# Sending the rows of maxima from ScalarE's queue, holding raw weights two tiles further ahead, and fixing the step of bulk loads, memory reads and input splits

## The chip, the cores and the metric

The kernel runs on one core of one Trainium2 chip. A core has five engines that run side by side and are ordered only by semaphores: TensorE (PE in the profile), VectorE (DVE), ScalarE (ACT), GpSimd (POOL) and SyncE (SP), which here issues DMAs. ScalarE has a DMA queue too. The metric is the device time of one execution in microseconds; lower is better.

## The reference

A gated sum of two branches over the same input `x` (2048 tokens of width 640, all float32): an attention with a compressive memory over four segments of 512 tokens, 32 heads of width 20, and a gated MLP of inner width 1728.

```python
g = sigmoid((x * gate_w).sum(-1, keepdims=True))
# branch a, for each segment s = 0..3, per head
p = softmax(qs @ ks.T * scale + mask)          # causal inside the segment
a_dot = p @ vs
a_mem = (phi(qs) @ M) / (phi(qs) @ z + 1e-6)   # phi(t) = t+1 if t>0 else exp(t)
o = sigmoid(beta) * a_mem + (1 - sigmoid(beta)) * a_dot
M, z = M + phi(ks).T @ vs, z + phi(ks).sum(rows)
a = concat(o) @ wo
# branch b
b = (silu(x @ w1) * (x @ w3)) @ w2
out = g * a + (1 - g) * b
```

## The kernel before, in words

**Numbers in parts.** Projections and MLP products keep near-float32 accuracy by splitting each operand into a high and a low part (`split`, line 110: ScalarE copies the high part, line 111, and VectorE or GpSimd subtracts for the low part, line 112) and doing three passes over each block of 128 columns (`PASSES`). For the attention scores, q and k are split into three bfloat16 parts (`parts`, line 246), stored to DRAM in the order that the score product wants, and loaded again two heads at a time.

**Dense work and attention side by side.** `attention()` is a generator that walks through 128 heads (4 segments of 32) and yields ten times for each head step `t`. In one step TensorE does the scores of head `t` (`s_unit`, three PSUM banks in turn, two buffers) for their row maxima, the transposed scores of head `t-3` (`st_unit`, tag `t`, two PSUM buffers), whose exp ScalarE takes straight from PSUM (line 565) and whose corner GpSimd masks (line 571), and for every fourth head the product with v (`pv_quad`). The scores of a pair of heads need their maxima as three extra rows of q: VectorE takes maxima (line 526), splits them into three parts (`max_parts`, lines 536 to 539), transposes them (`max_rows`, line 545), and a small DMA (line 546) writes them into rows 120 to 122 of the pair's q tile `qst`. The first transposed score of the pair (line 557), issued two head steps later, reads them.

The dense work (projections, MLP, memory, output product) is a list of generators, cut into segments with end steps `segs`. The main loop takes one step of the attention, adds the segment's mean cost per step to a credit, and runs dense steps, each of which yields its cost in ns, while the credit lasts. `braid(a, b, every, skip)` puts one step of `b` behind every so many steps of `a` and runs what is left of `b` at the end. `after(n, f)` runs `f` after `n` ticks; `tick()` is called ten times in a head step.

**Order on the engines.** TensorE runs exactly in program order. On every other engine and queue a planner orders the instructions by readiness in its own model of time, except those wrapped in `here(...)`, which are pinned behind the instruction of the same engine that stands just ahead of them in the program, and those pinned by `behind`. Each engine and each queue then works strictly in its order, so one that waits holds everything behind it.

**Weights.** All weights are a list of tiles of 128 x 640 in order of use. `w_load` (line 137) sends one from DRAM into one of two raw buffers (`NRAW = 2`, issue at line 141); `w_split` makes the two-part tile W in one of six buffers (`NW = 6`), ScalarE for the high part, GpSimd (VectorE for the first seven) for the low part. `clock["oldest"]` is the oldest tile still in use. After every dense step `w_step` may split the older raw tile once it is four or five steps old, and load the next one if its W would fit: `clock["next"] < oldest + NW`.

**The other names the change touches.** `split_x` (line 210) splits the input of segments 2 and 3 into X, five blocks of 512, one to a step. `load_pair` (line 492) loads q, k, and every eighth head v, for a pair three steps ahead. `o_sums` (line 594) starts, after a segment's last head, the load of the softmax sums (line 595), then `o_scale` (line 614), which inverts and splits them on VectorE and sends them to `rR`, and five `o_load`s (line 600), each several DMAs on SP, which fetch the attention output. `normalize` (line 636) multiplies it by the inverted sums and adds the memory's part (`gt`, from `load_memory`, line 628). `memory_read` (line 277) does the products `nd` of phi(q) with M in eight steps. `oproj` returns `first()`, five normalize steps and then the splits into `oT`, and `rest()`, the output product.

Of the kernel before, what the change touches and what calls it, by code (L numbers as in the profile page):

```python
# [17 lines left out]
P = 128  # L18
S, D, H, DH, NSEG, L = 2048, 640, 32, 20, 4, 512
# [3 lines left out]
VE = DH + 1  # L23
VG = 8 * VE
SCALE = DH ** -0.5
BIG = -1.0e38
NST, NW, NRAW, NHT, NVG, ND = 4, 6, 2, 6, 2, 3
KR = 6 * DH
LAG_T, LAG_P, NP, AGE, NO = 3, 4, 4, 4, 5
# [5 lines left out]
def gated_mix(ctx: ExitStack, tc: tile.TileContext, xT, wqk, wv, w13, w2, w2h, wo, beta, out):  # L35
    nc = tc.nc
# [8 lines left out]
    vd = [dp.tile([P, 4, H * VE], F32, name=f"vd{c}") for c in range(NSEG)]  # L45
# [51 lines left out]
    here = tc.keep_in_program_order  # L97
    last = {}
# [11 lines left out]
    def split(dst, src, lo=None, pin=lambda ins: ins):  # L110
        pin(nc.scalar.copy(dst[:, 0], src))  # L111
        (lo or nc.gpsimd.tensor_sub)(dst[:, 1], src, dst[:, 0].bitcast(F32))  # L112
# [4 lines left out]
    def ht_tile(shape, dt, name):  # L117
        return sp.tile(shape, dt, tag="hT", name=name, bufs=NHT)
# [10 lines left out]
    items, tiles = [], {}  # L129
# [21 lines left out]
    def w_step():  # L151


        clock["step"] += 1
        for r in raws:
            if clock["step"] - r[3] == (AGE // 2 if "exp" in last else AGE) and r[0] >= 7:
                r[4] = last.get("exp", last["act"])
        if raws and clock["step"] - raws[0][3] >= (AGE if "exp" in last or raws[0][0] < 7 else AGE + 1):
            w_split()
        if len(raws) < NRAW and clock["next"] < min(len(items), clock["oldest"] + NW):  # L160
            w_load()

    def w_get(i, oldest=None):
# [46 lines left out]
    def split_x(c):  # L210
        x_tile(c)
        for kb in range(KB):
            split(Xs[c][:, :, kb, :], xraw[c][kb], lo=nc.vector.tensor_sub)
            yield 1

    xraw = {}
# [29 lines left out]
    def parts(name, ps, phi=None):  # L246


        s = ht_tile([P, 3, L], BF, name)
        if phi is not None:  # L250
            e = f_tile("phi_t")
            nc.vector.tensor_scalar(e, ps, 0.0, None, op0=ALU.min)
        nc.scalar.copy(s[:, 0], ps)
        if phi is not None:
            nc.scalar.activation(e, e, AF.Exp)
        t = f_tile(f"{name}_t")
        nc.vector.tensor_sub(t, ps, s[:, 0])
        if phi is not None:
            nc.vector.scalar_tensor_tensor(phi, ps, 0.0, e, op0=ALU.max, op1=ALU.add)
        last["act"] = nc.scalar.copy(s[:, 1], t)  # L260
        nc.gpsimd.tensor_sub(s[:, 2], t, s[:, 1])
        return s
# [135 lines left out]
    def job_read(c):  # L398
        return 5.6, memory_read(c)
# [92 lines left out]
    def load_pair(j):  # L492

        c, h = divmod(j, H)
        q, k = qst[j // 2 % NST], kst[j // 2 % NST]
        for mb in {DH * h // P, (DH * h + 2 * DH - 1) // P}:
            assert ("q", c, mb) in stored and ("k", c, mb) in stored
        assert ("v", c, 3) in stored
        for t, src in ((q, qd[c]), (k, kd[c])):
            nc.sync.dma_start(t[:KR], src[DH * h:DH * h + 2 * DH].rearrange("(h d) a n -> (d a) h n", h=2))  # L500
        if h % 8 == 0:
            v = sp.tile([P, 4, VG + 12], F32, tag="vg", name=f"vg{j}", bufs=NVG)
            nc.gpsimd.memset(v[:, :, VG:], 0.0)
            nc.sync.dma_start(v[:, :, :VG], vd[c][:, :, VE * h:VE * h + VG])
            bank["v"] = v
        m = sp.tile([P, 8], F32, tag="m", name=f"m{j}", bufs=4)
        for i in range(2):
            o = VE * (h % 8 + i)
            heads[j + i] = dict(c=c, h=h + i, q=q[:, i], k=k[:, i], pair=q, v=bank["v"][:, :, o:o + 32], m=m)
# [32 lines left out]
    def max_rows(j):  # L542
        mr = sp.tile([32, P], BF, tag="mr", name="mr")
        for g in range(4):
            nc.vector.transpose(mr[:, 32 * g:32 * g + 32], heads[j]["ns"][32 * g:32 * g + 32])
        nc.sync.dma_start(heads[j]["pair"][KR:KR + 3].rearrange("a h (b n) -> a (h b) n", n=P), mr[:24])

    def st_unit(j, t):
        u = heads[j]
# [43 lines left out]

    def o_sums(c):
        here(nc.sync.dma_start(rs, od[c][:, DH].rearrange("h (a n) -> h a n", n=P)))
        after(4 if c < NSEG - 1 else 3, o_scale, c)
        for b in range(KB):
            after(1 + 3 * b if c < NSEG - 1 else 1 + b, o_load, c, b)

    def o_load(c, b):  # L600

# [26 lines left out]
    def load_memory(c):  # L628

        assert ("g", c, 3) in stored  # L630
        gms[c] = big_tile(f"gm{c}")[:, :4 * D].rearrange("p (b d) -> p b d", b=4)
        for qb in range(4):
            here(nc.sync.dma_start(gms[c][:, qb], gd[c][:, qb]))
            yield 1
# [20 lines left out]
    def after(n, f, *a):  # L655
        soon.append([n, f, a])
# [77 lines left out]
    def store(c, qb=None):  # L734
        o = out[0, c * L:(c + 1) * L, :].rearrange("(b p) d -> p b d", p=P)
        for qb in range(4):
            here(nc.sync.dma_start(o[:, qb], accs[c][:, qb]))
            yield 1
# [4 lines left out]
    def job_up(cs, j):  # L743
        return (4 if j < NF else 2) * 3.5, ffn_up(cs, j, plan_up([j])[0])
# [6 lines left out]
    def job_down(cs, g, last=False):  # L751
        return 2.384 * sum(3 if j < NF else 2 for j in GROUPS[g]), ffn_down(cs, GROUPS[g], plan_down(GROUPS[g]), last)

    def jobs_up(cs, g):
        return [job_up(cs, j) for j in GROUPS[g]]

    def jobs_group(cs, g):
        return [job_up(cs, j) for j in GROUPS[g]] + [job_down(cs, g)]
# [14 lines left out]
    def chain(jobs):  # L773
        return sum(c for c, _ in jobs), (y for _, g in jobs for y in g)

    def braid(a, b, every, skip=0):

        def gen():
            n = 0
            for y in a[1]:  # L780
                yield y
                n += 1
                if n > skip and (n - skip) % every == 0:
                    z = next(b[1], None)
                    if z is not None:
                        yield z
            yield from b[1]
        return a[0] + b[0], gen()

    A, B = (0, 1), (2, 3)  # L790
# [16 lines left out]

    seg = job_q2(A, 3)
    g = jobs_group(A, 0)
    seg += [braid(g[0], job_read(1), 2)] + g[1:] + jobs_group(A, 1) + jobs_up(A, 2)  # L810
    segs.append((H + LAG_P + 1, seg))
    d = job_down(A, 2)
    u = job_up(A, GROUPS[3][0])
# [8 lines left out]
    segs.append((2 * H - 3, seg))  # L822
    seg = job_q(B, 1) + job_q(B, 2)
    q = job_q2(B, 3)
    seg += q[:2] + [q[2], braid(q[3], job_read(2), 1)]
    segs.append((2 * H + LAG_P, seg))
    up = [job_up(B, 0), job_up(B, 1)]
    o1, o2 = jobs_oproj(1)
    seg = [braid(braid(up[0], job_read(3), 2), (0, load_memory(1)), 6), braid(up[1], o1, 2), o2, (0, store(1)), job_up(B, 2), job_down(B, 0)] + jobs_up(B, 1)
    segs.append((3 * H + LAG_P + 1, seg))  # L830
    d = job_down(B, 1)
    u = job_up(B, GROUPS[2][0])
    o1, o2 = jobs_oproj(2)
    seg = [braid(d, (0, load_memory(2)), 3), braid(u, o1, 2), o2] + [job_up(B, j) for j in GROUPS[2][1:]]
    seg += [job_down(B, 2), (0, load_memory(3))] + jobs_up(B, 3)
    segs.append((NJ + LAG_P, seg))
    d, u = job_down(B, 3), jobs_up(B, 4)
# [90 lines left out]
```

## Time and profile before

| | |
|---|---|
| median of 3 runs | 1187.81 us (1186.01 to 1189.77) |
| the profiled execution's own time | 1190.22 us |
| its span, first to last instruction | 1188.5 us |
| TensorE busy | 1151.5 us, 97% |
| VectorE / ScalarE / GpSimd busy | 681.0 / 495.0 / 458.1 us |
| mean granted TensorE clock | 0.991 |
| DMA | 151.87 MB, 128 GB/s on average |

How to read the lines that follow. Times are in us unless marked ns. A line of the waits names an engine and line of code, what it waited for, the us in total, how often, and the longest. A line of the order of time has start, length, engine, line, operation, output <- input and shape, and in brackets the idle time of that engine just before, and what ended it. A line of the stretches has the stretch, its length, then busy time and count of PE, PE's weight loads, VectorE, ScalarE and GpSimd, then the granted TensorE clock, the busy share of the DMA engines and GB/s. SPq is the queue of SP. TensorE's matmuls are pipelined, so a busy PE is not PE at its peak, but an idle one is idle. A wait for several semaphores is put down to the one that came last.

### The profile page before, as it was taken

The numbers are of one execution on the slowest core, as the hardware profiler recorded it, in microseconds if no ns is written. First come the engines' busy times: TensorE is split into PE (matmuls) and PEld (weight loads), VectorE is DVE, ScalarE is ACT, GpSimd is POOL, SyncE is SP. The second block draws the span as 40 slices with busy tenths as digits, with TensorE's granted clock in tenths as the row PEclk, the third lists the DMA queues.
The fourth block names the chain that finished last, engine by engine and source line by source line (L and its number), as shares of the span: only waits on it lengthen the run. The fifth ranks groups of instructions, "written<-read, shape, count | busy, mean of one in ns | idle before, by whom it ended". The sixth has DMA issues, their size and how long they took to land.

```text
span 1188.5 us, 20034 instructions
## 1 busy us (share of the span) xinstructions
PE 1151.5 (97%) x6953; PEld 875.6 (74%) x6953; DVE 681.0 (57%) x2183; ACT 495.0 (42%) x988; POOL 458.1 (39%) x574
## 2 busy tenths in 40 slices
PE   8999999999999999999999998999997999999998
PEld 6978766767767787877876665768666676776888
DVE  4033574466656655583365886765656776664454
ACT  6255334544342334343455633545542344334140
POOL 7065533244343335242265422342432325334250
PEclk9999999999999999999999999999998999999999
DMA  9375523233324244316377665342435324231212
GB/s 303 140 228 210 198 73 94 87 99 83 98 77 115 84 122 124 95 51 192 116 240 236 225 197 159 116 141 82 114 94 143 87 86 121 77 121 55 81 56 89
DMA packets 108213, 151.87 MB, mean 128 GB/s; under 512 B 12240, under 2 KB 69584, under 8 KB 108112
## 3 DMA queue, kind: packets, MB, share of 16 engines
q1 hardware_dynamic: 87760, 123.59, 34.7%
q10 hardware_dynamic: 20352, 27.01, 6.3%
q8 instruction: 54, 0.88, 0.3%
q14 instruction: 47, 0.39, 0.1%
HBM read 95.25 MB, written 54.53 MB: 126 GB/s over the span
## 4 chain that ended last, share of the span: by engine, by line
PE 82%; DVE 7%; DMA 4%; issue 3%; POOL 2%; ACT 1%; SPq 0%; POOLq 0%; DVEq 0%; ACTq 0%
PE g L224 15%; PE f L478 15%; PE u L224 14%; PE o L582 6%; PE v L325 6%; PE s L519 5%; PE op L718 5%; PE t L557 4%; PE k L224 4%; PE q L224 4%; DVE junk L526 2%; PE t L562 1%; DMA qst<-mr 1%; PE nd L291 1%; POOL W L112 1%
## 5 line engine op out<-in xcount | busy, mean ns | idle before, releaser
L526 DVE CUSTOM_DVE_ANT_0 junk<-s,mask 128x128 bf16<-128x128 f32 (+3 forms) x512 | 249.5, 487 | 220.7 <-PE s L519 213.0
L565 ACT ACTIVATE P<-t 128x384 f32<-128x384 f32 (+1 forms) x384 | 202.2, 527 | 351.7 <-PE t L557 137.7
L112 POOL TENSOR_TENSOR W<-wr,W 128x640 fp32r<-128x640 f32 (+1 forms) x126 | 197.2, 1571 | 171.2 <-ACT W L111 163.2
L571 POOL TENSOR_SCALAR_AFFINE_SELECT P<-P 128x256 f32<-128x256 f32 x256 | 105.1, 411 | 388.6 <-ACT P L565 377.4
L224 PE MATMUL g<-X,W 128*128 128x512 f32 x840 | 242.7, 424 | 0.0
L224 PE MATMUL u<-X,W 128*128 128x512 f32 x780 | 228.8, 429 | 1.0 <-DVE oall L643 1.0
L478 PE MATMUL f<-W,ht 128*128 128x320 f32 x1312 | 225.7, 323 | 2.9 <-DVE acc L483 2.6
L478 PEld LDWEIGHTS f<-W,ht 128*128 128x128 f32 x1312 | 201.7, 191 | 10.7 <-DVE acc L483 4.0
L224 PEld LDWEIGHTS g<-X,W 128*128 128x128 f32 x840 | 152.2, 190 | 26.8 <-issue 2.2
L224 PEld LDWEIGHTS u<-X,W 128*128 128x128 f32 x780 | 143.9, 192 | 25.6 <-DVE oall L643 1.4
L519 PE MATMUL s<-kst,qst 120*128 120x128 bf16 (+3 forms) x512 | 135.6, 306 | 1.2 <-DVE m L526 1.0
L111 ACT CAST W<-wr 128x640 fp32r<-128x640 f32 (+1 forms) x133 | 95.2, 724 | 67.9 <-PE f L478 21.7
L557 PE MATMUL t<-qst,kst 123*128 123x512 bf16 (+1 forms) x256 | 93.8, 366 | 10.4 <-DMA qst<-mr 9.6
L483 DVE SCALAR_TENSOR_TENSOR acc<-f,cgate,acc 128x320 f32<-128x320 f32 x128 | 70.0, 549 | 54.3 <-PE f L478 53.4
L112 POOL TENSOR_TENSOR ht<-ft,ht 128x512 fp32r<-128x512 f32 x52 | 67.8, 1304 | 74.5 <-ACT ht L111 73.7
L224 PE MATMUL q<-X,W 128*128 128x512 f32 x300 | 81.0, 414 | 3.7 <-POOL X L112 1.9
L519 PEld LDWEIGHTS <-qst 120*128 120x128 bf16 x512 | 44.3, 99 | 52.2 <-issue 44.2
L718 PE MATMUL op<-W,oT 128*128 128x320 f32 x480 | 82.7, 325 | 0.0
L224 PE MATMUL k<-X,W 128*128 128x512 f32 x300 | 80.7, 412 | 2.0 <-ACT mt L385 2.0
L325 PE MATMUL v<-W,X 128*128 128x320 f32 (+1 forms) x480 | 76.5, 317 | 1.8 <-POOL W L112 1.8
L582 PE MATMUL o<-P,vg 128*32 128x512 f32 (+3 forms) x1024 | 77.9, 443 | 0.3 <-POOL P L571 0.3
L718 PEld LDWEIGHTS op<-W,oT 128*128 128x128 f32 x480 | 73.8, 190 | 1.5 <-issue 0.4
(110 smaller groups left out, 1226.5 us busy)
## 6 DMA issues: line engine op xcount, KB each, us to landing
wr<-in_w_dram SPq DMA_DIRECT2D x80, 320.0 KB
qst<-qd SPq DMA_DIRECT2D x64, 240.0 KB
kst<-kd SPq DMA_DIRECT2D x64, 240.0 KB
od<-oq ACTq DMA_DIRECT2D x32, 256.0 KB
qd<-qs ACTq DMA_DIRECT2D x20, 384.0 KB
kd<-ks SPq DMA_DIRECT2D x20, 384.0 KB
wr<-in_wqk_dram SPq DMA_DIRECT2D x21, 320.0 KB
wr<-in_wo_dram SPq DMA_DIRECT2D x20, 320.0 KB
```

Of the source, the lines that this page charges most:

```text
L111: pin(nc.scalar.copy(dst[:, 0], src))
L112: (lo or nc.gpsimd.tensor_sub)(dst[:, 1], src, dst[:, 0].bitcast(F32))
L224: nc.tensor.matmul(ps, w[:, a, kb * P:(kb + 1) * P], x[:, b, kb, :], start=n == 0, stop=n == 14)
L325: nc.tensor.matmul(ps[:, :n1 - n0], x[:, a, kb, lb * P:(lb + 1) * P], wvt[kb][:, b, n0:n1], start=n == 0, stop=n == 14)
L478: nc.tensor.matmul(ps[:, :320], a, b, start=n == 0, stop=n == len(ms) - 1)
L519: nc.tensor.matmul(ps[:, o:o + n], q[:KR, qb * P:(qb + 1) * P], k[:KR, :n], start=qb != 1, stop=qb != 0, skip_group_check=True)
L526: nc.vector.tensor_tensor_reduce(out=junk[:, :n], in0=ps[:, o:o + n], in1=mask[:, L - n:], scale=1.0, scalar=-3.0e38, op0=ALU.add, op1=ALU ...
L557: nc.tensor.matmul(ps[:, :n], k[:KR + 3, t * P:(t + 1) * P], q[:KR + 3, t * P:], start=True, stop=True)
L565: last["exp"] = nc.scalar.activation(P32[:, o:o + n], src, AF.Exp, scale=SCALE)
L571: nc.gpsimd.affine_select(d, d, pattern=[[0, 2], [1, P]], base=0, channel_multiplier=-1, compare_op=ALU.is_ge, fill=0.0)
L582: nc.tensor.matmul(ps[32 * i:32 * i + 32, kb * P:], u["v"][:, kb], u["P32"][:, o:o + n], start=kb == 0, stop=kb == 3, skip_group_check=True)
L718: nc.tensor.matmul(ps[:, :320], oT[0][:, qb % 2, a, kb * P:(kb + 1) * P], ws[kb][:, b, 320 * hf:320 * hf + 320], start=n == 0, stop=n == 14)
```

## The change

- `max_rows`: the DMA of the rows is issued by ScalarE, pinned, six ticks after the transposes.
- `w_step`: raw tiles are loaded up to `NRAW` tiles beyond those whose W fits; the split now asks itself whether W fits.
- `split_x`: the ScalarE copies are pinned at their steps. `load_pair`: the loads of the first four pairs (`j < 8`) are pinned on SP.
- `parts`: ScalarE's copy stands ahead of VectorE's min in the program, for queries and keys with phi.
- `o_sums`: `o_scale` after 7 ticks, `o_load`s six ticks apart (first three segments).
- Segments: `job_read(1)` starts four steps later; `job_read(2)` leaves what does not fit to the next segment, whose first job takes it up ahead of `job_read(3)`, with another cost; `load_memory(1)` comes every five steps after eight; `load_memory(2)` moves ahead into the previous segment; `normalize(1)` starts two steps later and `normalize(2)` takes every third step in place of every second.

```diff
@@ w_step
-        if raws and clock["step"] - raws[0][3] >= (AGE if "exp" in last or raws[0][0] < 7 else AGE + 1):
+        if raws and raws[0][0] < clock["oldest"] + NW and \
+                clock["step"] - raws[0][3] >= (AGE if "exp" in last or raws[0][0] < 7 else AGE + 1):
             w_split()
-        if len(raws) < NRAW and clock["next"] < min(len(items), clock["oldest"] + NW):
+        if len(raws) < NRAW and clock["next"] < min(len(items), clock["oldest"] + NW + NRAW):
             w_load()
@@ split_x
-            split(Xs[c][:, :, kb, :], xraw[c][kb], lo=nc.vector.tensor_sub)
+            split(Xs[c][:, :, kb, :], xraw[c][kb], lo=nc.vector.tensor_sub, pin=here)
@@ parts
         s = ht_tile([P, 3, L], BF, name)
+        nc.scalar.copy(s[:, 0], ps)
         if phi is not None:
             e = f_tile("phi_t")
             nc.vector.tensor_scalar(e, ps, 0.0, None, op0=ALU.min)
-        nc.scalar.copy(s[:, 0], ps)
-        if phi is not None:
             nc.scalar.activation(e, e, AF.Exp)
@@ load_pair (q and k; the same for v)
-            nc.sync.dma_start(t[:KR], src[DH * h:DH * h + 2 * DH].rearrange("(h d) a n -> (d a) h n", h=2))
+            i = nc.sync.dma_start(t[:KR], src[DH * h:DH * h + 2 * DH].rearrange("(h d) a n -> (d a) h n", h=2))
+            if j < 8:
+                here(i)
@@ max_rows
-        nc.sync.dma_start(heads[j]["pair"][KR:KR + 3].rearrange("a h (b n) -> a (h b) n", n=P), mr[:24])
+        dst = heads[j]["pair"][KR:KR + 3].rearrange("a h (b n) -> a (h b) n", n=P)
+        after(6, lambda: here(nc.scalar.dma_start(dst, mr[:24])))
@@ o_sums
-        after(4 if c < NSEG - 1 else 3, o_scale, c)
+        after(7 if c < NSEG - 1 else 3, o_scale, c)
         for b in range(KB):
-            after(1 + 3 * b if c < NSEG - 1 else 1 + b, o_load, c, b)
+            after(1 + 6 * b if c < NSEG - 1 else 1 + b, o_load, c, b)
@@ braid
-    def braid(a, b, every, skip=0):
+    def braid(a, b, every, skip=0, rest=True):
...
-            yield from b[1]
+            if rest:
+                yield from b[1]
@@ segments
-    seg += [braid(g[0], job_read(1), 2)] + g[1:] + jobs_group(A, 1) + jobs_up(A, 2)
+    seg += [braid(g[0], job_read(1), 2, 4)] + g[1:] + jobs_group(A, 1) + jobs_up(A, 2)
...
-    seg += q[:2] + [q[2], braid(q[3], job_read(2), 1)]
+    r = job_read(2)
+    seg += q[:2] + [q[2], braid(q[3], r, 1, 0, False)]
...
-    seg = [braid(braid(up[0], job_read(3), 2), (0, load_memory(1)), 6), braid(up[1], o1, 2), o2, (0, store(1)), job_up(B, 2), job_down(B, 0)] + jobs_up(B, 1)
+    r = 0.37 * job_read(3)[0], chain([r, job_read(3)])[1]
+    seg = [braid(braid(up[0], r, 2), (0, load_memory(1)), 5, 8), braid(up[1], o1, 2, 2), o2, (0, store(1)), job_up(B, 2), job_down(B, 0), (0, load_memory(2))] + jobs_up(B, 1)
...
-    seg = [braid(d, (0, load_memory(2)), 3), braid(u, o1, 2), o2] + [job_up(B, j) for j in GROUPS[2][1:]]
+    seg = [d, braid(u, o1, 3), o2] + [job_up(B, j) for j in GROUPS[2][1:]]
```

More of the change, by code (lines that the diff above doesn't have):

```diff
@@ L503, in load_pair @@
             nc.gpsimd.memset(v[:, :, VG:], 0.0)
-            nc.sync.dma_start(v[:, :, :VG], vd[c][:, :, VE * h:VE * h + VG])
+            i = nc.sync.dma_start(v[:, :, :VG], vd[c][:, :, VE * h:VE * h + VG])
+            if j < 8:
+                here(i)
             bank["v"] = v
```

## The prediction

> **What bounds the kernel now.** I read the page first, then the waits of TensorE, then the granted clock around them, then the single instructions at each stall.
>
> ```profile
> span 1188.5 us, 20034 instructions
> PE 1151.5 (97%) x6953; PEld 875.6 (74%) x6953; DVE 681.0 (57%) x2183; ACT 495.0 (42%) x988; POOL 458.1 (39%) x574
> ```
>
> PE is busy for 97% of the span and the other engines for 57% at most. The matmuls are the same before and after, so the change can only win the time in which PE stands, or runs at half clock. TensorE's waits, longest first:
>
> ```profile
> PE t L557 <- DMA qst<-mr: 9.6, 2, 6.0
> PE f L478 <- DVE acc L483: 2.6, 2, 2.1
> PE nd L291 <- DVE fu L447: 2.6, 1, 2.6
> PE nd L291 <- DVE gm L299: 2.3, 2, 1.6
> ...
> PE v L325 <- POOL W L112: 1.8, 2, 1.2
> PE gt L647 <- DVE fu L447: 1.8, 2, 1.6
> ...
> PE s L519 <- DVE m L526: 1.0, 3, 0.7
> PE u L224 <- DVE oall L643: 1.0, 1, 1.0
> PE t L557 <- ACT P L565: 0.8, 1, 0.8
> ```
>
> These nine are 23.5 us. The largest is PE waiting for a row of maxima (mr) twice. Next, the busy time of the engines in five stretches; the figure before the last two is the granted clock:
>
> ```profile
> 526.30:529.70 3.40, 3.13 (x12) 3.13 (x13) 2.55 (x9) 0.73 (x1) 2.72 (x2) 0.50 0.32 94
> 703.80:707.20 3.40, 3.40 (x12) 2.41 (x12) 2.16 (x9) 0.93 (x2) 0.00 (x0) 0.50 0.68 200
> 720.90:724.30 3.40, 3.40 (x28) 1.17 (x24) 1.21 (x5) 0.00 (x0) 0.00 (x0) 0.50 0.81 281
> 912.00:918.80 6.80, 2.68 (x10) 2.41 (x11) 0.57 (x2) 0.00 (x0) 0.00 (x0) 0.50 0.98 262
> 942.70:946.10 3.40, 3.40 (x11) 2.29 (x10) 1.37 (x4) 0.38 (x1) 0.41 (x1) 0.51 0.27 88
> ```
>
> Each lies right behind (or over the end of) one of the stalls above. PE worked 3.13 + 3.40 + 3.40 + 2.68 + 3.40 = 16.0 us there at half clock, so 8.0 us were lost on top of the stalls. Stalls and half clock together, 31.5 us, are what this change could reach.
>
> **The change part by part.** The profiled execution took 1190.2 us, 2.4 above the median of the runs (1187.8); the sum is made against 1190.2 and 2.4 is taken off at the end.
>
> *Rows of maxima moved from SP's queue to ScalarE's.* The two late rows:
>
> ```profile
> 710.14 0.84 DVE L545 STREAM_TRANSPOSE mr<-ns 32x32 bf16<-32x32 bf16 x4
> 712.45 0.73 SPq L609 DMA_DIRECT2D oall<-od  x1
> 714.10 5.29 DMA qst<-mr
> 719.43 0.39 PE L557 MATMUL t<-qst,kst 123*128 123x512 bf16 x1 [3.59 <-DMA qst<-mr]
> 904.58 0.84 DVE L545 STREAM_TRANSPOSE mr<-ns 32x32 bf16<-32x32 bf16 x4
> 909.47 6.61 DMA qst<-mr
> 916.12 0.61 PE L557 MATMUL t<-qst,kst 123*128 123x512 bf16 x1 [6.03 <-DMA qst<-mr]
> ```
>
> The rows were ready at 710.98 and 905.42, but SP issued them at 714.10 and 909.47, behind a run of bulk loads. On ScalarE's queue they stand behind no bulk load. Their landing is bounded by two kinds of rows. The shortest from issue to first use:
>
> ```profile
> 741.96 0.72 SPq L546 DMA_DIRECT2D qst<-mr  x1
> 744.61 0.38 PE L557 MATMUL t<-qst,kst 123*128 123x512 bf16 x1
> ```
>
> is 2.65 us; with it both rows land at 713.6 and 908.1, before PE stood (715.84 and 910.09), and all 9.6 us go. With the 5.29 and 6.61 us of their own stretches they land at 716.27 and 912.03, 0.4 and 1.9 us remain, and 7.2 go. The bulk loads stay in those stretches, only thinner, so I take the middle, **8.4**. [...]
>
> The price is on ScalarE, which now issues 64 of them:
>
> ```profile
> L546 SPq DMA_DIRECT2D qst<-mr x64: 720/727/903, 151.1 to 1086.8; - x64
> 239.41 0.60 ACT L565 ACTIVATE P<-t 128x512 f32<-128x512 f32 x1 [1.03 <-POOL ht L112]
> 239.41 0.84 DVE L545 STREAM_TRANSPOSE mr<-ns 32x32 bf16<-32x32 bf16 x4
> 937.94 0.59 ACT L565 ACTIVATE P<-t 128x512 f32<-128x512 f32 x1
> 939.65 0.83 DVE L545 STREAM_TRANSPOSE mr<-ns 32x32 bf16<-32x32 bf16 x4
> ```
>
> 64 x 0.727 = 46.5 us of ScalarE's stream. Six ticks behind `max_rows` is the place right before the next `t` unit 0, so ScalarE issues the row before that unit's exp. I compared, for 63 pairs, that exp's start with the end of the transposes: in 26 of them (the first is the pair at 239) the rows are ready later, by 22.4 us in all and at most 2.5 us (940.48 against 937.94). In these ScalarE would stand, with that exp and everything behind it queued: the next exps, the tanh and the evacuations that VectorE waits for. Who needs that exp soonest is the matmul that takes its PSUM bank again, two units later:
>
> ```profile
> 653.36 0.60 ACT L565 ACTIVATE P<-t 128x512 f32<-128x512 f32 x1 [1.10 <-PE t L557]
> 657.20 0.23 PE L560 MATMUL t<-qst,kst 123*128 123x128 bf16 x1
> ```
>
> It has 657.20 - 653.96 = 3.2 us to spare, as much as the worst pair takes (2.5 + 0.73). So most is hidden. Ends: 0, and 26 x 0.73 + 22.4 = 41.4 if nothing hid it. PE waited for an exp once, for 0.8 us, so I stay near the lower end: **+3.0**. SP loses a wait: 64 rows no longer hold its queue, which delays nothing that PE waits for otherwise: 0.
>
> *X splits kept at set steps.* Five ScalarE copies of X3 now run in one burst when X's slot comes free, and the VectorE halves behind them hold back the evacuation:
>
> ```profile
> 521.59 2.78 DVE L112 TENSOR_TENSOR X<-xr,X 128x512 fp32r<-128x512 f32 x2
> 524.89 1.00 PE L478 MATMUL f<-W,ht 128*128 128x320 f32 x5 [2.14 <-DVE acc L483]
> ```
>
> With each copy pinned three steps after the last, two halves no longer meet. Between 0 and -2.6 I take the longer stall alone, **-2.1**.
>
> *Raw weights two tiles beyond.* 133 loads of 320 KB go up to two tiles earlier, and a split then follows as soon as its W slot is free, instead of load, five steps, split. The weights nearly never bind PE: 1.8 us for v, where five tiles are needed at once. **-1.8** (ends 0 and -1.8, and the row is that case).
>
> *`o_scale` at 7 ticks, `o_load`s six apart.* VectorE, in order, stood for the sums:
>
> ```profile
> DVE rs L616 <- DMA rs<-od: 4.5, 4, 1.7
> ```
>
> and the tanh product (fu), hence PE's 2.6 us for nd, came behind it. Three more ticks cover the 1.7: **-1.7** (ends 0, -2.6).
>
> *Memory reads later, memory loads earlier, normalize at every third step.* Starting `job_read(1)` four steps later removes the longer of the two gm waits: **-1.6** (ends 0, -2.3). Spacing `normalize(2)` wider removes gt and u, 2.8, in part: **-1.8**. But its `oT` splits then come at the very end of that up job, where before six steps lay between. The next product needs them:
>
> ```profile
> L111 ACT CAST oT<-oall x80: 287/297/325, 397.8 to 1163.5; 128x128 fp32r<-128x128 f32 x80
> ```
>
> The cost is between 0 and five copies and a VectorE half, about 1.8; the first matmul needs one copy behind one other ScalarE job, 0.3 + 0.6 + 0.3, so **+1.2**. `job_read(2)` leaves three of eight steps to the next segment but is paid in full in its own, so dense work ends some 2 us early there; an end without dense work cost PE the 0.8 (t) and 0.7 (s) above: **+0.8** (ends 0, 2.1). The next segment's pace is set 5.6 us too low and that work runs at its end; PE works either way: 0.
>
> *`parts`: ScalarE's copy before VectorE's min.* ScalarE no longer waits for phi_t in front of its exps; the t and s waits of 0.8 and 0.7 followed such a wait: **-1.5** (ends +0.8, -1.8). *Loads of the first four pairs pinned on SP*: nine transfers, with a lead of 30 ticks, 0.
>
> *Half clock.* 8.0 us, of which the stretches behind removed stalls go. **-5.0** (ends 0, -8.0), because not every stall goes. Here the half clock followed even the 2.1 us stall at 524.89. [...]
>
> *New order.* All engines but PE are planned anew, which can open waits like the 0.8 to 2.6 us ones above: **+3.0** (ends 0, 8).
>
> Sum: -8.4 - 2.1 - 1.8 - 1.7 - 1.6 - 1.8 - 1.5 - 5.0 = -23.9; +3.0 + 1.2 + 0.8 + 3.0 = +8.0; net -15.9. 1190.2 - 15.9 - 2.4 = **1172**.
>
> **The rivals.** *A, the small gains are given back.* VectorE's own delays stay:
>
> ```profile
> L537 DVE TENSOR_TENSOR nm<-m,ns x64: 103/168/1492, 147.5 to 1085.3; 128x8 f32<-128x8 f32 x64
> ```
>
> A 0.17 us operation took up to 1.49. The 126 weight splits on POOL remain, so the stalls of VectorE may only change place, and pins and steps do little. Then the rows alone gain: 8.4 + 3.0 of clock - 8.0 = 3.4, **1184**. Against it: four small stalls have an ordering cause that the change names. [...]
>
> *B, slower: ScalarE stands for the rows.* If the exp's 3.2 us of room is less elsewhere, all 41.4 us come to PE instead of 3.0: 1172 + 38 = **1210**. It decides from about 19 us exposed, under half of it. For it: 26 pairs come late. Against it: ScalarE is busy for 42%, and only one pair reaches the room.
>
> *C, slower: raw loads block SP.* A raw load waits for POOL to free the raw tile, with the next pairs' q and k behind it:
>
> ```profile
> SPq L141 <- POOL W L112: 186.7, 60, 16.1
> ```
>
> A pair is loaded three steps ahead, 22 us by the first and last start of the mr issues (935.7 / 63 = 14.9 us for two steps). If earlier loads double the longest wait, to 32, a pair is 10 late, with a half-clock stretch 11.7; three of them give **1207**. It decides from two such waits. Against it: today's longest is 6 us short of one.
>
> **How the numbers follow.** Forecast 0.54, with its own range 1163 to 1181; A 0.24; B 0.12; C 0.10. About 0.3% (1184.2 to 1191.4) is what a measurement of this kernel can tell from no change. A lies at that edge: 0.16 faster, 0.08 same. So faster 0.70, same 0.08, slower 0.22. Outside 1160 to 1198 lie B (0.12), half of C (0.05) and 0.03 below.
>
> **What would show it.** Right: PE's wait for mr under 2.4 us, no half clock at 720 and 912, PE's waits for acc and v gone, ScalarE's issues of mr near 0.73 us each. Wrong: exps standing behind mr (B), SP waiting over 22 us for POOL and PE for qst or kst (C), PE waits of the old total under other names (A).

## The result, and the profile after

| | before | after |
|---|---|---|
| median in the comparison | 1190.63 us (1186.01 to 1194.15) | 1179.38 us (1175.83 to 1180.61) |
| the profiled execution's own time | 1190.22 us | 1179.5 us |
| its span | 1188.5 us | 1177.5 us |
| mean granted TensorE clock in it | 0.991 | 0.996 |

The ratio after to before is 0.9903, with a 95% interval from 0.9875 to 0.9931: 11 us faster. The forecast was 1172, so the sign and the range held. The time is 7.4 us above the forecast, and 2.8 of these are no part of the change: the sum took 2.4 us off because the median of three runs was 1187.81, and over six runs the kernel before has 1190.63. Counted as a change, 15.9 us were forecast and 11.2 measured. From the page of the changed kernel, its span and the engines' busy time:

```profile
span 1177.5 us, 20041 instructions
...
PE 1148.4 (98%) x6953; PEld 874.2 (74%) x6953; DVE 684.9 (58%) x2183; ACT 495.5 (42%) x988; POOL 456.4 (39%) x574
```

The waits of TensorE in the changed kernel (what it waited for, us in total, how often, the longest):

```profile
PE t L562 <- DMA qst<-mr: 7.6, 4, 2.6
PE s L523 <- DVE m L530: 4.2, 4, 2.8
PE f L478 <- DVE acc L483: 1.4, 2, 0.9
...
PE nd L291 <- DVE gm L299: 1.2, 2, 0.7
PE u L225 <- DVE oall L648: 1.1, 2, 0.6
...
PE gt L652 <- DVE fu L447: 1.0, 1, 1.0
PE nd L291 <- DVE pq L259: 0.9, 1, 0.9
PE v L325 <- ACT W L111: 0.8, 1, 0.8
...
PE t L565 <- ACT P L570: 0.4, 1, 0.4
PE t L562 <- ACT P L570: 0.4, 2, 0.2
```

The two long waits for a row of maxima (3.6 and 6.0 us) are gone, but four short ones stand in their place, and together they are 7.6 us against 9.6. The waits for `fu` ahead of `nd` (2.6) and for GpSimd's weights ahead of `v` (1.8) are gone; the wait for the maxima ahead of the scores (`s`) rose from 1.0 to 4.2. The stretches of half clock in the changed kernel (busy times, then the granted clock ahead of the last two figures):

```profile
641.50:645.00 3.50, 3.50 (x12) 2.02 (x10) 1.43 (x6) 0.49 (x1) 0.57 (x2) 0.51 0.58 185
709.80:713.30 3.50, 3.50 (x19) 1.75 (x22) 1.66 (x6) 0.00 (x0) 0.00 (x0) 0.51 0.75 219
750.80:754.20 3.40, 3.40 (x11) 1.97 (x9) 0.89 (x4) 0.60 (x1) 0.00 (x0) 0.50 0.19 75
```

10.4 us against 20.4 us before (the five stretches of the prediction, each with its full length): of those the first lies behind the `s` wait, the other two behind rows of maxima.

The rows come late now for two reasons. Two of the three long waits, near 707 and 748, look like this in the order of time:

```profile
704.16 0.84 DVE L549 STREAM_TRANSPOSE mr<-ns 32x32 bf16<-32x32 bf16 x4
705.03 0.73 ACTq L551 DMA_DIRECT2D qst<-mr  x1
...
708.68 0.39 PE L562 MATMUL t<-qst,kst 123*128 123x512 bf16 x1 [1.96 <-DMA qst<-mr]
...
745.73 0.83 DVE L549 STREAM_TRANSPOSE mr<-ns 32x32 bf16<-32x32 bf16 x4
746.60 0.73 ACTq L551 DMA_DIRECT2D qst<-mr  x1
...
750.60 0.43 PE L562 MATMUL t<-qst,kst 123*128 123x512 bf16 x1 [2.55 <-DMA qst<-mr]
```

No queue holds these rows: they are ready at 705.00 and 746.56 and are issued within 0.04 us. But TensorE wants them at 706.72 and 748.05, that is 1.7 and 1.5 us after they are ready. In the kernel before, the two late rows were ready 4.9 and 4.7 us ahead of TensorE's need (710.98 against 715.84, 905.42 against 910.09), and it was SP's queue that used this up. Now VectorE makes the rows late. The last of the four waits has another cause:

```profile
897.50 0.34 SPq L500 DMA_DIRECT2D qst<-qd  x1
...
898.81 0.90 DVE L549 STREAM_TRANSPOSE mr<-ns 32x32 bf16<-32x32 bf16 x4
...
903.26 0.73 ACTq L551 DMA_DIRECT2D qst<-mr  x1
904.09 1.50 ACT L570 ACTIVATE P<-t 128x512 f32<-128x512 f32 x3 [5.48 <-DMA wr<-in_wo_dram]
...
909.18 0.39 PE L562 MATMUL t<-qst,kst 123*128 123x512 bf16 x1 [2.62 <-DMA qst<-mr]
```

The row is ready at 899.71 and nothing stands ahead of it on ScalarE, but ScalarE issues it only at 903.26. From 898.12 on its queue stands for 5.1 us at a wait for two semaphores. One of them is raised by SP's load of a later pair (issued at 897.50), and its last update comes at 903.19, just before the row goes out; the profile puts the time down to a load of raw weights. Neither is of the row's own pair. In this trace all 490 DMAs of SP and all 152 of ScalarE raise the same eight completion semaphores, and the row raises the one of the load at 897.50: it goes out at 903.26, 0.07 us after that load's last update. So the row has left SP's queue and still waited for one of SP's loads. Three exps stood behind it.

### The profile page after: what moved, and what is told of

Read it like the earlier page. It is cut to its first block, busy times and chain, and to the rows that moved or that the text cites. A ratio compares the mean times of both kernels' runs of the same rounds, so it can differ in the third digit from the quotient of the medians.

```text
span 1177.5 us, 20041 instructions
## 1 busy us (share of the span) xinstructions
PE 1148.4 (98%) x6953; PEld 874.2 (74%) x6953; DVE 684.9 (58%) x2183; ACT 495.5 (42%) x988; POOL 456.4 (39%) x574
## 4 chain that ended last, share of the span: by engine, by line
PE 80%; DVE 7%; issue 5%; DMA 5%; ACT 1%; POOL 1%; SPq 0%; POOLq 0%; ACTq 0%; DVEq 0%
PE f L478 16%; PE g L225 14%; PE u L225 14%; PE o L587 6%; PE s L523 5%; PE q L225 5%; PE op L723 5%; PE k L225 4%; PE t L562 4%; PE v L325 3%; DMA wr<-in_wqk_dram 2%; DVE junk L530 2%; DMA qst<-mr 2%; PE pm L381 1%; PE t L567 1%
## 5 line engine op out<-in xcount | busy, mean ns | idle before, releaser
L478 PEld LDWEIGHTS f<-W,ht 128*128 128x128 f32 x1312 | 199.2, 189 | 9.5 <-DVE acc L483 2.6
```

The source lines that it names most:

```text
L478: nc.tensor.matmul(ps[:, :320], a, b, start=n == 0, stop=n == len(ms) - 1)
```

## The experiments

In the figures, "mr", "s", "fu", "pq", "v" are TensorE's waits in the profiled execution, in us, for rows of maxima, for the maxima ahead of the scores, for the tanh product ahead of `nd`, for the phi product ahead of `nd`, and for the weights ahead of `v`. Likewise "acc" is the wait for the sum of the MLP ahead of `f`, "gm" for the memory's result ahead of `nd`, "gt" for the tanh product ahead of `gt`, "u" for the normalized output, and "k" for a copy of ScalarE ahead of `k`. "Before" ran beside each group at 1188.18 to 1190.63 us.

**1. The rows alone.** The kernel before, with one edit:

```diff
-        nc.sync.dma_start(heads[j]["pair"][KR:KR + 3].rearrange("a h (b n) -> a (h b) n", n=P), mr[:24])
+        dst = heads[j]["pair"][KR:KR + 3].rearrange("a h (b n) -> a (h b) n", n=P)
+        after(6, lambda: here(nc.scalar.dma_start(dst, mr[:24])))
```

> The kernel before (1190.6 us) with only the rows of maxima moved to ScalarE's queue, six ticks later. Theory R (the prediction's: the move of the rows carries about half of the gain, 8.4 us less 3.0 for ScalarE): 1183 to 1187, and PE's wait for mr down from 9.6 to under 3 us. Theory S (the steps carry it; the rows gain nothing because ScalarE now stands in front of them, for VectorE or for a transfer): 1188 to 1194, with PE's wait for mr still over 5 us.

Measured: 1177.35 us, ratio 0.9903 [0.9886, 0.992]. That is the whole change's gain from one edit, and 6 us better than theory R's range, though its figure for mr came true. TensorE's waits in this kernel:

```profile
PE f L478 <- DVE acc L483: 2.6, 2, 2.1
PE nd L291 <- DVE fu L447: 2.4, 1, 2.4
PE nd L291 <- DVE gm L299: 2.3, 2, 1.6
PE t L558 <- DMA qst<-mr: 2.3, 1, 2.3
```

mr fell from 9.6 to 2.3, by 7.3 us, just inside the lower of the two bounds, 7.2 and 9.6. The other waits stay as they were before, the wait for exps (0.8) among them. The range took off 3.0 us for ScalarE that were not paid, and left out half clock: the profile of this kernel has one stretch of 3.4 us, against 20.4 us before.

**2. Everything but the rows.** The changed kernel, with the rows sent by SP as before:

```diff
-        dst = heads[j]["pair"][KR:KR + 3].rearrange("a h (b n) -> a (h b) n", n=P)
-        after(6, lambda: here(nc.scalar.dma_start(dst, mr[:24])))
+        nc.sync.dma_start(heads[j]["pair"][KR:KR + 3].rearrange("a h (b n) -> a (h b) n", n=P), mr[:24])
```

> The changed kernel (1179.4 us) with the rows of maxima back on SP's queue. Theory R: 1184 to 1188, the two late rows back. Theory S: 1177 to 1181, no worse than the changed kernel, because the spread bulk loads alone let SP issue the rows in time.

Measured: 1176.16 us, ratio 0.9894 [0.9879, 0.9908]; mr 5.0 in three waits, the longest 4.2; s 5.0. Theory R fell, and theory S came, with a little more: the other parts alone gain as much as the rows alone, 13.4 us here, 12.2 in the first experiment, 11.2 together. The gains don't add. The row near 900 leaves SP's queue 0.03 us after it is ready (900.16 and 900.19), where it stood there for 4.05 us before, so both edits remove the longest stall (6.0). The row near 705 still stands for 2.1 us on SP's queue (704.00 and 706.08), and TensorE waits 4.2 us for it, against 3.6 before. Which of the other parts cleared the queue near 900 was not separated.

**3. Everything but the raw weights.** Both conditions of `w_step` as before:

```diff
-        if raws and raws[0][0] < clock["oldest"] + NW and \
-                clock["step"] - raws[0][3] >= (AGE if "exp" in last or raws[0][0] < 7 else AGE + 1):
+        if raws and clock["step"] - raws[0][3] >= (AGE if "exp" in last or raws[0][0] < 7 else AGE + 1):
-        if len(raws) < NRAW and clock["next"] < min(len(items), clock["oldest"] + NW + NRAW):
+        if len(raws) < NRAW and clock["next"] < min(len(items), clock["oldest"] + NW):
```

> The changed kernel with raw weights loaded, as before, only when their W fits. The prediction gave this part 1.8 us, for v alone: 1180 to 1183, and PE's wait for W in the v product back at about 1.8 us. Rival: the earlier raw loads do more than v shows (SP free of them in the bursts): 1185 or more. Second rival: they only crowd SP and the transfers: 1176 or less.

Measured: 1184.14 us, ratio 0.996 [0.9945, 0.9976]. v came back as expected (1.8), but the time rose by 4.8 us, a little over the range. TensorE's waits change in other places too: fu 3.8, pq 2.6, k 1.8, with mr down to 5.7 and s to 1.8. In the profile TensorE stands idle for 31.2 us against 29.1, only 2.1 more; the rest goes with half clock, five stretches against three. Why waits so far from `v` move was not tested; the splits of raw weights on GpSimd and ScalarE, and VectorE's order behind them, are the likely way.

**4. Everything but the set steps.** X splits not pinned, `o_scale` at 4, `o_load`s three apart, and the four edits of segments undone:

```diff
-            split(Xs[c][:, :, kb, :], xraw[c][kb], lo=nc.vector.tensor_sub, pin=here)
+            split(Xs[c][:, :, kb, :], xraw[c][kb], lo=nc.vector.tensor_sub)
-        after(7 if c < NSEG - 1 else 3, o_scale, c)
+        after(4 if c < NSEG - 1 else 3, o_scale, c)
-            after(1 + 6 * b if c < NSEG - 1 else 1 + b, o_load, c, b)
+            after(1 + 3 * b if c < NSEG - 1 else 1 + b, o_load, c, b)
...
```

> The changed kernel with the X splits unpinned and o_scale, o_load, the memory reads and loads and normalize at the steps of the kernel before; rows, raw loads, parts and pair pins as changed. Theory S: 1187 to 1191, with half-clock stretches back at the X split, at the tanh product near 700 and at normalize of the third segment. Theory R: 1181 to 1185.

Measured: 1179.86 us, ratio 0.9912 [0.9893, 0.9931], level with the whole change and better than both theories had it. acc 2.8 and fu 3.2 are back as expected, and so, in the profiled execution (the slowest of the six), is half clock near 525, 706 and 935. But mr is down to 0.9: what the steps win at acc, fu and gt (5.4 together) they lose at mr (6.7).

**5. Rows on GpSimd's queue.** The changed kernel, with `nc.gpsimd.dma_start` in place of `nc.scalar.dma_start`.

> The changed kernel (1179.4 us) with the rows of maxima issued by GpSimd's queue at the same step. In the changed kernel ScalarE stood 5.1 us at 898 in front of a row that was ready, and three exps behind it. Theory Q (it stood for a load on SP's queue that had landed late and that its transfer has to follow; a queue that SP's loads share nothing with does not): PE's wait for mr down from 7.6 to under 3 us and 1173 to 1178 us. Rival (rows are late wherever they are issued, and GpSimd's weight splits of 1.57 us make it worse): PE's wait for mr 7 us or more, 1180 us or more.

Measured: 1177.25 us, ratio 0.9908 [0.9881, 0.9936]; mr 7.9 in five waits. Neither theory holds whole: mr is the rival's, the time theory Q's. The wait at 906 went: GpSimd's DMAs raise eight semaphores of their own in this trace, and the row goes out 0.3 us after it is ready. The waits near 705 and 745 stayed (1.7 and 2.6), though these rows too go out within 0.4 us, and three new ones (0.7, 1.2 and 1.8) came, ending at 722, 782 and 797. ScalarE is not what makes the rows late at 705 and 745.

**6. Everything but `parts`.** The copy behind the min again:

```diff
-        nc.scalar.copy(s[:, 0], ps)
         if phi is not None:
             e = f_tile("phi_t")
             nc.vector.tensor_scalar(e, ps, 0.0, None, op0=ALU.min)
+        nc.scalar.copy(s[:, 0], ps)
+        if phi is not None:
             nc.scalar.activation(e, e, AF.Exp)
```

> The changed kernel with ScalarE's copy in parts between VectorE's min and the exp again, as before. Theory P (the new order of parts brought the wait of s for the maxima, 2.8 us at 637, where the prediction had it take 1.5 us away): PE's wait for s falls from 4.2 to under 2 us, no half clock at 641, 1175 to 1178 us. Rival (the prediction's: parts gains 1.5): 1180 to 1182 us, the wait unchanged.

Measured: 1181.45 us, ratio 0.9946 [0.9927, 0.9966]: `parts` is worth some 2 us, as the rival said, though the intervals overlap. The first theory fell: s is 3.4, not under 2. The gain is at another place than either had it: pq 3.9 against 0.9. In the order of time of this kernel, GpSimd and VectorE ahead of that wait, and the wait:

```profile
674.79 1.16 POOL L262 TENSOR_TENSOR qs<-qs_t,qs 128x512 bf16<-128x512 f32 x1 [2.45 <-ACT qs L261]
...
676.28 1.55 POOL L112 TENSOR_TENSOR W<-wr,W 128x640 fp32r<-128x640 f32 x1
```

```profile
675.21 0.76 DVE L541 CAST ns<-m 128x8 bf16<-128x8 f32 x1
...
676.36 1.50 DVE L543 CAST ns<-nm 128x8 bf16<-128x8 f32 x1
...
680.68 0.68 DVE L260 SCALAR_TENSOR_TENSOR pq<-q,phi_t 128x512 f32<-128x512 f32 x1
```

```profile
681.41 1.73 PE L292 MATMUL nd<-Ms,pq 128*128 128x84 f32 x6 [3.92 <-DVE pq L260]
```

The two casts end when GpSimd's operations end (675.97 against 675.95, 677.86 against 677.83). In the changed kernel the same cast falls ahead of GpSimd's split, which starts at 676.84 there:

```profile
675.67 0.17 DVE L542 CAST ns<-nm 128x8 bf16<-128x8 f32 x1
```

0.17 us against 1.50, so this one operation makes up 1.3 of the 3.0 us; the rest was not traced. The kernel before has such rows too: the nine longest of VectorE's operations that write `nm` or `ns` (1.42 to 1.50 us) each start within one of GpSimd's weight splits and end 0.02 to 0.03 us after it. What ties the two engines together there is not shown. TensorE's wait for exps is 1.0 us here and 0.8 in the changed kernel, so freeing the exps accounts for little of the gain; `parts` helped by where VectorE's order happens to fall.

**7. Rows, raw weights, X pins, `o_scale` and the first memory read.** The kernel before with these five, without `parts`, the wide `o_load`s and the other segment steps:

```diff
+        if raws and raws[0][0] < clock["oldest"] + NW and \
...
+        if len(raws) < NRAW and clock["next"] < min(len(items), clock["oldest"] + NW + NRAW):
...
+            split(Xs[c][:, :, kb, :], xraw[c][kb], lo=nc.vector.tensor_sub, pin=here)
...
+        after(6, lambda: here(nc.scalar.dma_start(dst, mr[:24])))
...
+        after(7 if c < NSEG - 1 else 3, o_scale, c)
...
+    seg += [braid(g[0], job_read(1), 2, 4)] + g[1:] + jobs_group(A, 1) + jobs_up(A, 2)
```

> The kernel before with five parts of the change alone: rows on ScalarE's queue, raw weights two tiles beyond, X splits pinned, o_scale at 7 ticks, the first memory read four steps later. If gains add up (each of these took its own stall away and the others of the change brought new ones): 1169 to 1174 us. If every new order opens stalls of the size it closes: 1176 to 1180 us, as the kernels so far.

Measured: 1183.7 us, ratio 0.995 [0.9931, 0.9969]. Both expectations fell: this is 6 us slower than the rows alone. mr is 0.4, acc 1.4 and gm 0.7, all as they should be, but s rose to 5.4, pq to 3.9, fu to 3.1, and v kept 1.6, now for ScalarE. These edits each remove the wait that they aim at, and as much opens elsewhere.

**8. Every row sent twice.** The kernel of experiment 1, where ScalarE sends each row a second time, to DRAM that nothing reads: 64 DMA issues more and nothing else.

```diff
+    spare = [dp.tile([3, 2, L], BF, name=f"spare{i}") for i in range(64)]
-        after(6, lambda: here(nc.scalar.dma_start(dst, mr[:24])))
+        dst2 = spare[j // 2].rearrange("a h (b n) -> a (h b) n", n=P)
+        after(6, lambda: (here(nc.scalar.dma_start(dst, mr[:24])), here(nc.scalar.dma_start(dst2, mr[:24]))))
```

> The run with the rows alone moved (1177.4 us), each row sent twice by ScalarE, the second time to a place in DRAM that nobody reads: 64 more issues of about 0.73 us on ScalarE's queue, 46.7 us. Theory of the prediction (ScalarE has room, 3.0 us for the first 64 issues): 1177 to 1183 us. Rival B (what ScalarE spends comes to PE): 1195 us or more. Third: if the issues are wholly hidden, 1175 to 1178 us.

Measured: 1176.61 us, ratio 0.9897 [0.9874, 0.992], no slower than with one, which is the third case. The view of the rows in this kernel (durations in ns: shortest, median, longest; then who waited for them, us and times):

```profile
L549 ACTq DMA_DIRECT2D qst<-mr x64: 728/729/1363, 151.8 to 1072.3; - x64
L549 ACTq DMA_DIRECT2D spare<-mr x64: 302/456/668, 153.2 to 1073.1; - x64
...
  ACT P L568: 12.6, 9
  ACT W L112: 7.4, 2
  ACT qs L254: 4.5, 2
```

ScalarE issues for another 64 x 0.456 = 29 us (an estimate by the median) and stands for 12.6 + 7.4 + 4.5 = 24.5 us in waits that the landing of a row ended. TensorE's wait for exps rises from 0.8 to 1.9, but the time does not. So the price of a second 64 issues is not measurable, and in experiment 1, with the first 64, the wait for exps is the 0.8 of before.

**9 to 11. Which steps bring the rows late again.** The changed kernel, in 9 with the `o_load`s three apart and all four edits of segments undone (the X pins, `o_scale` at 7 and the rest kept); in 10 with the `o_load`s three apart alone; in 11 with the segments' edits undone from `job_read(2)` on (the wide `o_load`s kept).

```diff
-            after(1 + 6 * b if c < NSEG - 1 else 1 + b, o_load, c, b)
+            after(1 + 3 * b if c < NSEG - 1 else 1 + b, o_load, c, b)
```

```diff
-    r = job_read(2)
-    seg += q[:2] + [q[2], braid(q[3], r, 1, 0, False)]
+    seg += q[:2] + [q[2], braid(q[3], job_read(2), 1)]
-    r = 0.37 * job_read(3)[0], chain([r, job_read(3)])[1]
-    seg = [braid(braid(up[0], r, 2), (0, load_memory(1)), 5, 8), braid(up[1], o1, 2, 2), o2, (0, store(1)), job_up(B, 2), job_down(B, 0), (0, load_memory(2))] + jobs_up(B, 1)
+    seg = [braid(braid(up[0], job_read(3), 2), (0, load_memory(1)), 6), braid(up[1], o1, 2), o2, (0, store(1)), job_up(B, 2), job_down(B, 0)] + jobs_up(B, 1)
-    seg = [d, braid(u, o1, 3), o2] + [job_up(B, j) for j in GROUPS[2][1:]]
+    seg = [braid(d, (0, load_memory(2)), 3), braid(u, o1, 2), o2] + [job_up(B, j) for j in GROUPS[2][1:]]
```

> The changed kernel without its new segment steps and with o_loads three ticks apart, so: rows, raw loads, parts, pair pins, X pins and o_scale at 7 ticks. Theory T (the new segment steps and the wide o_loads brought PE's waits for mr at 706, 747 and 906 back; X pins and o_scale take their own stalls away): PE's wait for mr under 3 us, no stall over 2 us at 522 or 701, 1171 to 1176 us. Rival (each new order opens as much as it closes): 1177 us or more.

> The changed kernel with the o_loads three ticks apart again. Theory C (ScalarE's 5.1 us stand in front of a ready row at 898 comes from sharing a completion semaphore with a load that the wide o_loads put there): the stall of 2.6 us at 906 goes, another row may be hit, PE's wait for mr 5 us or less. Rival (ScalarE stands there in any case): wait for mr 7 us or more, the stall at 906 stays.

> The changed kernel with the second memory read finished in its own segment, the second segment's normalize and memory load at the old steps, and the third's too. Theory D (the row at 747 is late because the changed steps put the oT splits of VectorE between that pair's maxima and its transposes): the stall of 2.6 us at 747 goes, 1175 to 1178 us. Rival (the stall stays, since weight splits on GpSimd hold VectorE there): 1179 us or more.

Measured:

| kernel | us | ratio, 95% interval | mr | s | fu | gt <- fu |
|---|---|---|---|---|---|---|
| 9, both undone | 1177.14 | 0.989 [0.9869, 0.9911] | 2.0 | 5.7 | 3.4 | 1.8 |
| 10, `o_load`s undone | 1178.33 | 0.9907 [0.9881, 0.9934] | 5.0 | 4.2 | 1.6 | 1.0 |
| 11, segments undone | 1175.06 | 0.9886 [0.986, 0.9911] | 0.9 | 6.2 | 3.2 | 1.8 |
| the change | 1179.38 | 0.9903 [0.9875, 0.9931] | 7.6 | 4.2 | 0 | 1.0 |

TensorE's waits in 11:

```profile
PE s L523 <- DVE m L530: 6.2, 7, 2.8
PE nd L291 <- DVE fu L447: 3.2, 1, 3.2
...
PE gt L652 <- DVE fu L447: 1.8, 2, 1.6
...
PE t L562 <- DMA qst<-mr: 0.9, 1, 0.9
```

In 9 the wait for rows is under 3 us as the theory had it, but fu stands at 3.4 near 699 and the time is the rival's. In 10 and 11 the stalls at 906 and 747 go as expected.

The segments' edits account for most of the rows' lateness (7.6 to 0.9) and take away fu and part of gt and s: they trade 3.2 + 0.8 + 2.0 us against 6.7. Without the wide `o_load`s the wait at 906 shrinks to 0.3: there ScalarE stands 2.99 us instead of 5.48, and the row is issued at 899.89.

Near 705 the two waits are largely one. In 11 VectorE stands 2.3 us for the softmax sums (line 621, at 697.09), the tanh product is behind that, and TensorE waits 3.2 us for it; the row that follows is then 0.9 us late. In the changed kernel the tanh product goes ahead of the sums (695.57 against 697.66), TensorE doesn't wait for it, and the work on the sums falls between the pair's last maximum (700.64) and its transposes (704.16), 3.5 us against 1.5 in 11. As far as these rows show, fu comes back as mr.

Kernel 11 has the lowest median of all, 4 us under the change, but the intervals overlap, so that it beats the change is not shown.

## Why the prediction was right, and where its size was off

The sign, the range and two of the causes are the forecast's: fewer stalls (TensorE idle for 29.1 us in the profile, against 37.0) and less half clock. The size came out near by luck in part, since errors of both signs met in the sum. Of the signs that the prediction set for being right, one came in full (ScalarE's issues of mr at 0.73 us), and half clock is gone at 720 and 912 but stands at 710 and 751. The other two did not come: mr is 7.6 and not under 2.4, and 1.4 of acc and 1.2 of v are left. Point by point, with the term in the sum and what was measured:

- **Rows of maxima, -8.4.** Alone nearly right: -7.3 (experiment 1). In the whole change it is -2.0 (9.6 to 7.6), and this is the term that was mis-sized most, by 6.4 us. I priced the late rows by the queue and by the transfers around them in the profile before; the time from issue to use that I took (2.65 to 6.61 us) held, with 3.65 and 4.00 at 705 and 747. Two steps failed. "On ScalarE's queue they stand behind no bulk load": one row does, through the completion semaphore (5.1 us at 898). And I took it for granted that a row is ready as long ahead of TensorE's need as before (4.9 and 4.7 us); in the changed kernel it is 1.7 and 1.5 at the other two, because VectorE does other work between the maxima and the transposes: near 705 the softmax sums, whose delay showed as fu before, and near 747 the normalize steps and `oT` splits of the segments' edits.
- **ScalarE's price, +3.0.** Too high: experiment 8 doubles the issues at no measurable cost. Rival B (ScalarE stands for the rows) falls. This error offset half of the one on the rows.
- **X splits, -2.1.** -1.2 (acc 2.6 to 1.4; without the pins 2.6 to 2.8 in experiments 1, 4 and 8). The longer stall went, a part of 0.9 stayed.
- **Raw weights, -1.8.** The wait for GpSimd's `v` went, 0.8 for ScalarE and 0.4 for VectorE came. But the edit does more by reordering: undone alone it costs 4.8 us, and in experiment 7, where it stands beside the rows with the X pins and two of the steps but without `parts`, the result is 6 us slower than the rows alone.
- **`o_scale` and `o_load`s, -1.7.** The step failed: VectorE's wait for the sums is 4.5 us in all, as before, with a longest one of 2.8 against 1.7. fu went by 2.6, but not by `o_scale`: with it at 7 ticks fu is 3.4 in 9, 3.2 in 11 and 1.6 in 10. It was the segments' edits, with the wide `o_load`s, that moved `fu`.
- **`job_read(1)`, -1.6.** gm 2.3 to 1.2, but 4 and 9, without the step, have 1.2 as well. The step as such is not shown to have done it.
- **`normalize`, -1.8; `oT`, +1.2.** gt and u went from 2.8 to 2.1, gt by 0.8 and u not. No wait of the output product came.
- **The carried read, +0.8; `parts`, -1.5; new order, +3.0.** The `s` wait rose by 3.2, mostly one stall of 2.78 at 640. That stall is there without the carried read too (2.8 in 9 and 11). It is 1.8 without the raw weights (3), 2.0 without `parts` (6), and 0.7 where neither is in (before and experiment 1). So it is the new order and not the carry: the size of that term is right by luck. `parts` had the right size at another place, by luck too. Not in the sum at all are k, q and pq, which fell by 1.3, 0.9 and 0.7 us.
- **Half clock, -5.0.** In the profiled executions TensorE worked 16.0 us at half clock before and 10.4 after, so 8.0 - 5.2 = 2.8 went (an estimate by the granted clock of 0.50 to 0.51). Over several executions the means are (the clock is recorded to 0.001, so one product is good to about 0.6 us):

| kernel (executions) | mean span, us | mean granted clock | span x clock, us |
|---|---|---|---|
| before (17) | 1186.9 | 0.9929 | 1178.5 |
| the change (6) | 1177.0 | 0.9960 | 1172.3 |
| rows alone (5) | 1175.8 | 0.9964 | 1171.6 |
| no raw weights, experiment 3 (6) | 1182.7 | 0.9918 | 1173.1 |
| experiment 11 (4) | 1174.2 | 0.9955 | 1168.9 |

By this measure 6.2 of the 9.9 us of the change are stalls and 3.7 (1186.9 - 1178.5 less 1177.0 - 1172.3) the clock; in the profiled pair TensorE's idle time falls by 7.9 us. Forecast were 10.9 and 5.0. The measure is rough, since it counts a stall inside a half-clock stretch by half. The 4.8 us of experiment 3 are mostly clock: its product is 0.8 over the change's.

**Rival A** (small gains are given back) is half true. The change gained 11.2 us and not 3.4, but the rows alone gain as much, and everything added to them gives back what it wins. Its sign, the old total of waits under other names, is there in part: all that the view lists are 25.4 us against 32.8. Giving back should have been a term of the sum as large as the gains of the small steps together. Rival C (raw loads block SP) did not come: SP's longest wait for GpSimd is 15.5 us against 16.1, though the waits sum to 236.0 against 186.7.

## What to carry to other kernels

Where an engine other than the bound one is planned anew by every edit, price each removed stall alone, and then expect stalls to come back under other names. Even a large one with a named cause (here rows behind bulk loads) was worth 7.3 us alone and 2.0 beside the other edits. Ask of each stall that stays how long its cause is ready ahead of need: a stall that is removed in front of it uses that time up. A DMA that is moved to another engine's queue can still stand for a load of the first one: here a row on ScalarE's queue stood 5.1 us at a wait for a semaphore that a load of SP raised, and on GpSimd's queue, whose DMAs raised eight others, it went out 0.3 us after it was ready. Look at what the issuing engine waits for, not only at what is ahead of the DMA. Where half clock follows stalls, as in the three stretches (10.4 us) of the changed kernel, compare span times granted clock next to the time. Two executions of one kernel here (experiment 4) lay 7.7 us apart with products within 0.6 us of each other, where the whole change is 11.

## What the runs showed of the hardware that was not expected

- **The same stall was followed by half clock in two kernels (2.14 us before, 2.13 in experiment 8) and not in a third (2.13 in experiment 1).** The profile before had half clock behind the 2.14 us stall at 524.89, and the prediction names that row for its term. The kernels of experiments 1 and 8 have the same stall (2.13 us, at 525.15 and 525.81). In every kept trace with more than one, the half-clock stretches start whole multiples of 3.413 us apart (before: 526.31, 703.80, 720.87, 912.02, 942.74, which is 52, 5, 56 and 9 times that; after: 641.58, 709.85, 750.81, 20 and 12 times). With each trace divided into windows on that grid, the window that holds the stall and the next one, in the kernel before, in experiment 1 (where the stall falls into two windows) and in experiment 8:

```profile
522.90:526.31 3.41, 1.18 (x6) 0.84 (x6) 3.41 (x4) 0.76 (x2) 3.41 (x3) 1.00 0.36 96
526.31:529.72 3.41, 3.15 (x12) 3.15 (x13) 2.56 (x9) 0.73 (x1) 2.71 (x2) 0.50 0.32 95
```

```profile
521.08:524.49 3.41, 1.94 (x12) 1.33 (x10) 3.41 (x6) 2.85 (x6) 2.53 (x3) 1.00 0.00 1
524.49:527.91 3.42, 2.25 (x13) 1.85 (x14) 3.42 (x8) 0.73 (x1) 3.39 (x3) 1.00 0.35 96
527.91:531.32 3.41, 3.41 (x24) 3.17 (x24) 3.04 (x8) 0.49 (x1) 1.85 (x2) 1.00 0.58 165
```

```profile
523.52:526.93 3.41, 1.28 (x7) 0.85 (x6) 3.41 (x4) 1.06 (x2) 3.41 (x3) 1.00 0.31 91
526.93:530.34 3.41, 2.92 (x12) 2.85 (x12) 2.79 (x9) 0.73 (x1) 2.98 (x2) 0.50 0.28 77
```

  TensorE is busy for 1.18 and 1.28 of 3.41 us where half clock follows, and for 1.94 and 2.25 where it doesn't. I divided all thirteen traces in this way, from 20 to 1150 us. Of the windows at full clock, all 31 with TensorE busy for under 47% are followed by half clock, 4 of the 12 between 47% and 52.5%, and none of the 4220 above. So in these traces half clock came only behind windows with TensorE busy for 52.5% or less, and how a stall of 2 to 3 us fell on the grid made the difference: the longest of those for rows in the changed kernel, 2.62 us at 909.18, falls into two windows (busy 1.83 and 2.05 us), and no half clock followed. Which of the stalls that were removed would have paid is therefore partly luck, and so is the size of the half-clock term. In experiment 4 two executions of one kernel had spans of 1172.6 and 1180.3 us at clocks of 0.998 and 0.991. Half clock followed stalls of 2.1 to 2.8 us here (2.14 before 526.31 in the kernel before, 2.78 before 641.58 in the changed one).
- **64 more DMA issues on ScalarE cost no measurable time here,** nor do the 24.5 us that ScalarE stands still with them (experiment 8: 1176.61 against 1177.35 us).
- **A DMA issue stood 5.1 us for a transfer of another engine's queue,** at a wait for a completion semaphore that both raise (the changed kernel at 898.12). With the rows on GpSimd's queue, whose DMAs raise eight other semaphores in the trace of experiment 5, that row goes out 0.3 us after it is ready.
